# A long convolution feeding soft-MoE slots: the second stage's tables loaded whole at the start, its first loads half a step sooner, and wider scaled copies in the filter pass

## The chip, the core and the metric

One core of a Trainium2 chip runs the whole program. A time is the device time of that core in microseconds (us), from one execution. TensorE (PE) multiplies matrices into PSUM, ScalarE (ACT) and VectorE (DVE) read PSUM, GpSimd (POOL) adds and subtracts in SBUF, and SyncE (SP) issues nearly all DMA transfers of this kernel, in the order in which the program lists them. ACT issues four small loads at the start.

## What is computed

```python
x (8, 5696, 128), h (5696, 128)
Yf = rfft(x, 2S) * rfft(h, 2S)          # along the sequence
y  = irfft(Yf)[:, :S, :]                # causal long convolution per channel
x  = y.reshape(45568, 128)
logits = x @ phi                         # 32 slots
slot_input = softmax(logits, 0).T @ x    # per slot, over all tokens
slot_out   = relu(slot_input @ w1[e]) @ w2[e]      # 8 experts, 4 slots each
out = softmax(logits, 1) @ slot_out
```

All of it is float32. The filter `h` and the eight batches of `x` pass through the same forward transform: the filter is treated as group 0 and the batches as groups 1 to 8.

## The kernel before, in words

The transform of each group is done as two matrix stages with a transpose through DRAM between them. Three pipelines run side by side, each a number of steps behind the one before it. A step is one turn of the loop `for t in range(last_front + 1)` (line 547); there are 8 steps to a group (`NJ = 8`), and 72 steps of the first stage.

**Stage A** (lines 204-219) multiplies a folded piece of the input by the table `s1`. `load_x` (line 178) brings a piece of 4 x 2 columns with two DMAs into one of three buffers (`xcs`). `fold` (line 195) has POOL add or subtract the two halves into `x0` or `x1`. `stage_a(t, comp)`, called with `comp` 0 and 1 in each step, does two products into two PSUM banks out of a ring of four (line 211), ACT evicts both into `fst` (line 213; three such buffers, so a fourth eviction needs the store of the first to have landed), and SP stores `fst` to the DRAM tensor `f_g` with two DMAs (line 217). A float32 product shows as two MATMUL rows in the trace, so one `stage_a` is four rows. Each step issues four stores of `f` (180 KB each by the page) and one load of x.

**Stage B** begins nine steps after stage A (`LAG_B = NJ + 1`) and works in units of two rows of tables: 23 units to a group, up to three to a step, called from `slot_b` (line 561). `load_g(u)` (line 224) loads 256 KB of `f` into one of five `gt` buffers. `stage_b1(u)` (line 235) multiplies it by its slices of the table `wt` into a PSUM tile `bt` of two banks, `a = 0` and `a = 1` (line 244). For groups 1 to 8 DVE multiplies that by the filter's transform (`Hr`, `Hi`) into `pr`, `pi`, and adds them into `yf` (lines 265-270, two `yf` buffers). `stage_b2` (line 274) multiplies `yf` by the table `vt` into `bz`, ACT evicts into `zst`, SP stores to `z`.

For group 0, the filter, `stage_b1` takes another branch (lines 249-263). For each half `a`, ACT makes two scaled copies `ph` (128 x 128 each, one for each component `c`, line 253) from PSUM into a buffer, `pr` for `a = 0` and `pi` for `a = 1`, one of each; DVE then adds PSUM times a scale to each of them, giving `Hr` (line 255) and `Hi` (line 258). POOL negates `Hi` (line 261). The unit's PSUM tile is `bt` or `bz` by the parity of the unit; the next unit of the same parity needs both DVE halves to be through.

**Stage C** (lines 309-456) starts at step 27 and does the inverse transform's second half, the logits, both softmaxes and the slot sums. After the loop a tail handles the last pieces and the experts.

The order of the work is written out by hand (`manual_schedule`): within one step, PE, ACT, DVE, POOL and SP each get their instructions in the order of the calls: table pieces (lines 571-576), `stage_a(t, 0)`, `fold(t+1, 0)`, a unit, a unit, `load_x(t+3)`, `stage_a(t, 1)`, `fold(t+1, 1)`, a unit. `prefetch(last)` (line 554) issues the loads of `f` that are allowed: up to unit `last`, and none of group g before step 8g + 8, when all its stores have been issued. Calls in `slot_b` keep four units ahead; the very first call is at the end of step 8 (line 624).

The tables `wt` (128 x 45 x 64 float32, 1.47 MB) and `vt` (128 x 23 x 2 x 64 float32, 1.51 MB) are brought in slices of 6 and 3 rows, one slice a step: `wt` from step 7 to 14 and `vt` from step 15 to 22 (line 576), each of about 192 KB.

Of the kernel before, what the change touches and what calls it, by code (L numbers as in the profile page):

```python
# [10 lines left out]
F32 = mybir.dt.float32  # L11
AF = mybir.ActivationFunctionType
# [62 lines left out]
def kernel(  # L75
# [24 lines left out]
    nc = tc.nc  # L100
    P = 128
    B, S, D = x.shape
# [5 lines left out]
    R1, HALF, NP = S // N2, N2 // 2, N1 // 2  # L108
    CH = 4
    NJ = HALF // CH  # L110
    NU = (NP + 1) // 2
# [10 lines left out]
    t_s1, t_i1, t_w, t_v, t_turn = [  # L122
        nc.inline_tensor(t, f"tab_{n}").ap()
        for n, t in zip(("s1", "i1", "w", "v", "turn"), transform_tables(S, N1, N2, CH, X0, F0, F1))]
# [33 lines left out]
    bpool = front.enter_context(tc.tile_pool(name="bpool", bufs=1))  # L158

    s1 = apool.tile([P, 3, P], F32, name="s1", tag="s1", bufs=1)  # L160
    wt = fconst.tile([P, NP, HP], F32, name="wt")
    vt = fconst.tile([P, NU, 2, HP], F32, name="vt")
    turn = fconst.tile([P, 2, NU, 2], F32, name="turn")
# [14 lines left out]
    def load_x(c):  # L178
        if c >= (B + 1) * NJ:
            return  # L180
        g, j = divmod(c, NJ)
        src = (h if g == 0 else x[g - 1]).rearrange("(a n) d -> a n d", n=N2)
        t_ = xcs[c % len(xcs)]
        gap = N2 - CH * (2 * j + 1)
        for r in (slice(0, SPLIT), slice(SPLIT, R1)):
            v = src[r, CH * j:CH * (j + 1), :]
            v = bass.AP(tensor=v.tensor, offset=v.offset,
                        ap=[v.ap[0], [gap * D, 2], [1, CH * D]])
            nc.sync.dma_start(
                out=t_[X0 + r.start:X0 + r.stop, :, :, :].rearrange("p s n d -> p s (n d)"), in_=v)  # L190
        xs[c] = t_
# [43 lines left out]
    def stage_b1(u):  # L235
        g, i = divmod(u, NU)
        n = min(2, NP - 2 * i)
        t_ = gs.pop(u)
        tag = "bz" if g == 0 and i % 2 else "bt"
        bt = bps.tile([P, 2, 512], F32, name="bt", tag=tag)  # L240
        for a in range(2):
            r = slice(a * HP, (a + 1) * HP)
            for q in range(n):
                nc.tensor.matmul(bt[q * HP:(q + 1) * HP, a, 0:2 * D], wt[r, 2 * i + q, :],  # L244
                                 t_[r, q, :, :].rearrange("p c d -> p (c d)"),
                                 start=True, stop=True)
        r = slice(0, n * HP)
        pv = bt[r, :, 0:2 * D].rearrange("p a (c d) -> p a c d", c=2)
        if g == 0:
            for a in range(2):  # L250
                pr = bpool.tile([P, 2, D], F32, name="ph", tag="pi" if a else "pr")
                for c in range(2):
                    nc.scalar.activation(pr[r, c, :], pv[:, a, c, :], AF.Copy,  # L253
                                         scale=turn[r, 0, i, a:a + 1])
                nc.vector.scalar_tensor_tensor(  # L255
                    out=Hr[r, i, a, :], in0=pv[:, a, 1, :], scalar=turn[r, 1, i, a:a + 1],
                    in1=pr[r, 0, :], op0=AL.mult, op1=AL.add)
                nc.vector.scalar_tensor_tensor(
                    out=Hi[r, i, a, 0, :], in0=pv[:, a, 0, :], scalar=turn[r, 1, i, a:a + 1],
                    in1=pr[r, 1, :], op0=AL.mult, op1=AL.subtract, reverse1=True)  # L260
            nc.gpsimd.tensor_scalar(out=Hi[r, i, :, 1, :], in0=Hi[r, i, :, 0, :], scalar1=-1.0,
                                    scalar2=None, op0=AL.mult)
            return
        pr, pi = [bpool.tile([P, 2, 2, D], F32, name=f"p{c}", tag=f"p{c}") for c in "ri"]
        nc.vector.tensor_tensor(out=pr[r, :, :, :], in0=pv,  # L265
                                in1=Hr[r, i, :, :].unsqueeze(2).broadcast_to([n * HP, 2, 2, D]),
                                op=AL.mult)
        nc.vector.tensor_tensor(out=pi[r, :, :, :], in0=pv, in1=Hi[r, i, :, :, :], op=AL.mult)  # L268
        y_ = bpool.tile([P, 2, 2, D], F32, name="yf", tag="yf", bufs=2)
        nc.vector.tensor_tensor(out=y_[r, :, :, :], in0=pr[r, :, :, :], in1=pi[r, :, ::-1, :],  # L270
                                op=AL.add)
        prods[u] = y_
# [247 lines left out]
    LAG_B, LAG_C = NJ + 1, 3 * NJ + 3  # L520
    PER = -(-NU // NJ)
# [11 lines left out]
    AHEAD = 4  # L533
# [3 lines left out]
    nc.scalar.dma_start(out=s1[:, :, :], in_=t_s1)  # L537
    for c in range(1, 3):
        load_x(c)
    nc.scalar.dma_start(out=phi[:, :], in_=moe_phi)  # L540
    nc.scalar.dma_start(out=turn[:, :, :], in_=t_turn)
    nc.scalar.dma_start(out=i1[:, :, :], in_=t_i1)
# [4 lines left out]
    for t in range(last_front + 1):  # L547
        us = list(units(t))

        def pair(lag):  # L550
            T, half = divmod(t - LAG_C - lag, 2)
            return T if half == 0 and 0 <= T < NT else None

        def prefetch(last):
            nonlocal loaded
            while loaded < len(queue) and queue[loaded][0] <= last \
                    and queue[loaded][0] // NU * NJ + NJ <= t:
                load_g(queue[loaded][0])
                loaded += 1

        def slot_b():
            fresh = bool(us)
            if fresh:
                u = us.pop(0)
                prefetch(u + AHEAD)
                stage_b1(u)
                wait_b2.append(u)
            if len(wait_b2) > fresh:
                stage_b2(wait_b2.pop(0))

        for tab, src, first, n, k in ((wt, t_w, LAG_B - 2, NP, 2 * PER),
                                      (vt, t_v, LAG_B + NJ - 2, NU, PER)):
            p0 = k * (t - first)
            if 0 <= p0 < n:
                v = slice(p0, min(n, p0 + k))
                nc.sync.dma_start(out=tab[:, v], in_=src[:, v])
        if t < NA:
            stage_a(t, 0)
            fold(t + 1, 0)
        if pair(3) is not None:  # L580
            dispatch(pair(3))
        slot_b()
        T, U = pair(0), pair(2)
        if t == last_front:
            assert T is None and U is None and not us[1:]
            slot_b()
            stage_c2(pair(1))
            slot_b()
            assert not us and not wait_b2
            V = pair(1)  # L590
            stage_c6(V - 2)
            stage_c3(V)
            column_max(V)
            break
        rows = (lambda: None) if U is None else (lambda: stage_c4(U))
        after = None
        if T is not None:
            after = stage_c1(T, rows)
        else:
            rows()  # L600
        if pair(1) is not None:
            stage_c2(pair(1))
        if pair(5) is not None:
            stage_c6(pair(5))
        slot_b()
        if pair(-2) is not None:
            load_pair(pair(-2))
        if t < NA:
            load_x(t + 3)
        if after:  # L610
            after()
        if U is not None:
            stage_c5(U)
        if t < NA:
            stage_a(t, 1)
            fold(t + 1, 1)
        if pair(1) is not None:
            stage_c3(pair(1))
        slot_b()
        if pair(1) is not None:  # L620
            column_max(pair(1))
        if U is not None:
            softmax(U)
        if t == NJ:
            prefetch(AHEAD)
        if t == NA:
            lead.close()
            wts = inner.enter_context(tc.tile_pool(name="wts", bufs=1, side="right"))
            w1s = wts.tile([P, E, F], F32, name="w1s")
        if NA < t <= NA + E:  # L630
            nc.sync.dma_start(out=w1s[:, t - NA - 1, :], in_=moe_w1[t - NA - 1])
# [12 lines left out]
                      in_=zring[0][gap, :, :, :, :, :].rearrange("k h o n c d -> k (h o n c d)"))  # L644
# [14 lines left out]
    for q in range(Q):  # L659
        r = slice(q * NSL, (q + 1) * NSL)  # L660
        nc.gpsimd.tensor_copy(out=rep4[r, :, :],
                              in_=ident[r, r].unsqueeze(1).broadcast_to([NSL, Q, NSL]))
# [17 lines left out]
    for V in range(T, NT):  # L680
# [30 lines left out]
        else:  # L711
            for i in range(4 * (V - T - 1), min(4 * (V - T), E), 2):
                nc.sync.dma_start(
                    out=w2s[:, i:i + 2, :, :],
                    in_=moe_w2[i:i + 2].rearrange("e (p c) d -> p e c d", p=P))
# [28 lines left out]
    for g in range(EG):  # L744
        for f0 in range(0, F, FH):
# [5 lines left out]
            src = p[:, :].rearrange("p (c k) -> p k c", k=NFC)  # L751
# [5 lines left out]
    for g in range(EG):  # L757
        for k0 in range(0, NFC, 4):
            p = bank()
            for k in range(4):  # L760
# [3 lines left out]
                out=hidT[:, g, k0:k0 + 4, :], in_=p[:, :].rearrange("p (k c) -> p k c", k=4))  # L764
# [28 lines left out]
    for b in range(B):  # L793
        for w0 in range(0, NV, G4):
            n = min(G4, NV - w0)
# [10 lines left out]
            for q in range(Q):  # L806
                dst = o_[:, 0:n + lone, q, :]
                src = pq[q][:, 0:(n + lone) * D].rearrange("p (k d) -> p k d", d=D)
# [41 lines left out]
```

## Time and profile before

| what | value |
|---|---|
| median of 6 runs | 961.31 us (952.73 to 964.51) |
| the profiled execution's own time | 964.51 us |
| its span, first to last instruction | 962.7 us |
| PE busy | 849.7 us (88%) |
| DVE busy | 670.6 us (70%) |
| ACT busy | 522.3 us (54%) |
| POOL busy | 445.9 us (46%) |
| DMA | 272.51 MB, 283 GB/s over the span |
| share of the 16 DMA engines, SP's queue | 89.0% |
| first unit of stage B starts | 53.18 us |
| first unit of group 1 starts | 112.86 us |

The times in the rows below are us from the first instruction; durations in brackets after a row are how long its engine sat idle before it, and what ended that. "SPq" rows are SP issuing a DMA, not the transfer. The DMA share is the mean busy share of the 16 DMA engines. The line numbers are those of the kernel listed above.

### The profile page before, as it was taken

The page shows a single profiled execution, that of the slowest core. Times are in us where ns is not written, and L with a number is a line of the kernel's source. Part 1 is how long each engine was busy: PE and PEld are TensorE (multiplying, and loading weights), DVE is VectorE, ACT ScalarE, POOL GpSimd, SP SyncE. Part 2 cuts the span into 40 slices and gives each one's busy share as a digit, 9 for nine tenths or more (in the row PEclk, how much of TensorE's full clock was granted, in tenths as well). Part 3 has the DMA queues.
Part 4 walks back from the last instruction along what each step waited for, and adds up shares of the span by engine and source line. Part 5 has one row for each costly group of instructions (what it writes and reads, how often), then busy time and mean ns, then how long its engine had stood idle before and what let it go on. Part 6 is the DMA issues. An engine that isn't in the chain of part 4 may idle for free.

```text
span 962.7 us, 20396 instructions
## 1 busy us (share of the span) xinstructions
PE 849.7 (88%) x7220; PEld 408.0 (42%) x7220; DVE 670.6 (70%) x1140; ACT 522.3 (54%) x1068; POOL 445.9 (46%) x408
## 2 busy tenths in 40 slices
PE   6867788899899999999999899999998876787893
PEld 2322233334344444444444344444443333344883
DVE  3034577577778787888888688888889995573552
ACT  3556544455466566666665466656654444374442
POOL 5646533245465455555555555666533342462000
PEclk9979999999999999999999999999999998787865
DMA  6989899999999999999999999999989886742698
GB/s 179 277 264 265 269 311 325 308 309 288 275 290 287 298 312 300 332 297 301 315 313 275 276 312 307 311 287 321 306 275 311 276 280 194 226 162 117 235 406 334
DMA packets 174239, 272.51 MB, mean 283 GB/s; under 512 B 14982, under 2 KB 119686, under 8 KB 171253
## 3 DMA queue, kind: packets, MB, share of 16 engines
q1 hardware_dynamic: 173563, 270.86, 89.0%
q8 instruction: 58, 0.95, 0.4%
q10 hardware_dynamic: 576, 0.36, 0.2%
q14 instruction: 42, 0.34, 0.1%
HBM read 142.85 MB, written 128.21 MB: 282 GB/s over the span
## 4 chain that ended last, share of the span: by engine, by line
PE 70%; DMA 17%; issue 3%; DVE 3%; POOL 2%; SPq 1%; ACT 1%; DVEq 0%; ACTq 0%; POOLq 0%
PE bank L211 23%; PE bank L336 12%; PE bt L244 12%; PE bz L284 8%; DMA gt<-f 5%; PE bank L364 4%; DMA out_dram<-o 4%; DMA f<-fst 3%; DMA zd<-z 3%; PE bank L449 2%; PE bank L402 2%; PE bank L373 2%; POOL y L355 2%; PE bank L425 2%; PE bank L473 1%
## 5 line engine op out<-in xcount | busy, mean ns | idle before, releaser
L211 PE MATMUL bank<-x,s 128*128 128x512 f32 x576 | 285.7, 623 | 10.0 <-POOL x L200 7.9
L200 POOL TENSOR_TENSOR x<-xc 128x512 f32<-128x512 f32 x144 | 183.4, 1274 | 149.6 <-PE bank L211 83.0
L213 ACT ACTIVATE fst<-bank 128x512 f32<-128x512 f32 x288 | 167.9, 597 | 98.7 <-PE bank L211 68.0
L288 ACT ACTIVATE zst<-bz 128x512 f32<-128x512 f32 (+1 forms) x184 | 108.2, 588 | 171.6 <-PE bz L284 161.2
L265 DVE TENSOR_TENSOR pr<-bt,Hr 128x512 f32<-128x512 f32 (+1 forms) x184 | 126.9, 689 | 105.9 <-PE bt L244 102.8
L244 PE MATMUL bt<-gt,wt 64*64 64x256 f32 x1620 | 138.7, 405 | 53.4 <-DMA gt<-f 19.5
L270 DVE TENSOR_TENSOR yf<-pr,pi 128x512 f32<-128x512 f32 (+1 forms) x184 | 154.0, 837 | 6.4
L211 PEld LDWEIGHTS bank<-x,s 128*128 128x128 f32 x576 | 100.3, 193 | 133.1 <-issue 88.3
L268 DVE TENSOR_TENSOR pi<-bt,Hi 128x512 f32<-128x512 f32 (+1 forms) x184 | 125.0, 679 | 0.0
L284 PE MATMUL bz<-yf,vt 64*64 64x256 f32 x1440 | 117.3, 385 | 6.2 <-DVE yf L270 4.2
L336 PE MATMUL bank<-zc,i 128*64 128x512 f32 x480 | 118.8, 618 | 1.3 <-issue 1.3
L244 PEld LDWEIGHTS bt<-gt,wt 64*64 64x64 f32 x1620 | 44.7, 132 | 170.0 <-PE bank L211 53.5
L355 POOL TENSOR_TENSOR y<-y,op 128x512 f32<-128x512 f32 x64 | 77.4, 1210 | 70.7 <-DVE op L341 68.0
L355 POOL TENSOR_TENSOR y<-y,om 128x512 f32<-128x512 f32 x54 | 76.2, 1411 | 2.1
L410 POOL MEMSET dt<- 64x8 f32 x32 | 3.4, 106 | 157.2 <-ACT dn L413 84.3
L284 PEld LDWEIGHTS bz<-yf,vt 64*64 64x64 f32 x1440 | 54.0, 134 | 42.8 <-issue 11.6
L255 DVE SCALAR_TENSOR_TENSOR Hr<-bt,turn,ph 128x128 f32<-128x128 f32 (+1 forms) x46 | 16.1, 349 | 75.6 <-ACT ph L253 75.6
L364 PE MATMUL bank<-ident,y 109*128 109x109 f32 x512 | 60.0, 272 | 2.1 <-POOL y L355 1.4
L364 PEld LDWEIGHTS bank<-ident,y 109*128 109x128 f32 x512 | 52.5, 148 | 14.9 <-issue 11.6
L366 ACT ACTIVATE yt<-bank 128x360 f32<-128x360 f32 x128 | 51.9, 472 | 4.8 <-PE bank L364 4.8
L336 PEld LDWEIGHTS bank<-zc,i 128*64 128x64 f32 x480 | 30.0, 138 | 54.5 <-issue 48.6
L803 PE MATMUL op<-so,cT 32*128 32x128 f32 x704 | 46.8, 375 | 4.3 <-ACT o L812 3.7
(97 smaller groups left out, 896.4 us busy)
## 6 DMA issues: line engine op xcount, KB each, us to landing
f<-fst SPq DMA_DIRECT2D x288, 180.0 KB
gt<-f SPq DMA_DIRECT2D x198, 256.0 KB
z<-zst SPq DMA_DIRECT2D x176, 256.0 KB
zc<-z SPq DMA_DIRECT2D x30, 1024.0 KB
xc<-in_x_dram SPq DMA_DIRECT2D x64, 320.0 KB
out_dram<-o SPq DMA_DIRECT2D x16, 1024.0 KB
zc<-z SPq DMA_DIRECT2D x30, 416.0 KB
out_dram<-o SPq DMA_DIRECT2D x8, 768.0 KB
```

The lines of the kernel that those rows point to most:

```text
L200: nc.gpsimd.tensor_tensor(out=y_[:, :, :], in0=t_[:, 0, :, :], in1=t_[:, 1, ::-1, :], op=AL.subtract if comp else AL.add)
L211: nc.tensor.matmul(p[:, :], s1[:, tab[G], :], src[:, :, :].rearrange("p n d -> p (n d)"), start=True, stop=True)
L213: nc.scalar.activation(st[:, :, G, :], p[:, :].rearrange("p (n d) -> p n d", d=D), AF.Copy)
L244: nc.tensor.matmul(bt[q * HP:(q + 1) * HP, a, 0:2 * D], wt[r, 2 * i + q, :], t_[r, q, :, :].rearrange("p c d -> p (c d)"), start=True, sto ...
L265: nc.vector.tensor_tensor(out=pr[r, :, :, :], in0=pv, in1=Hr[r, i, :, :].unsqueeze(2).broadcast_to([n * HP, 2, 2, D]), op=AL.mult)
L268: nc.vector.tensor_tensor(out=pi[r, :, :, :], in0=pv, in1=Hi[r, i, :, :, :], op=AL.mult)
L270: nc.vector.tensor_tensor(out=y_[r, :, :, :], in0=pr[r, :, :, :], in1=pi[r, :, ::-1, :], op=AL.add)
L284: nc.tensor.matmul(bz[a * HP:(a + 1) * HP, q, 0:2 * D], vt[r, i, a, :], y_[r, a, :, :].rearrange("p c d -> p (c d)"), start=True, stop=True)
L288: nc.scalar.activation(st[:, 0:n, :], bz[:, 0:n, 0:2 * D], AF.Copy)
L336: nc.tensor.matmul(p[h_ * HP:(h_ + 1) * HP, :], i1[0:kr, tab, :], t_[0:kr, h_, o, :, q, :], start=True, stop=True)
L355: eng.tensor_tensor(out=part_, in0=part(v, 0), in1=o_[:, :, :], op=sign)
L364: nc.tensor.transpose(p[:, i * TR:(i + 1) * TR], ys[T][0:TR, k * CH + i, 0:D], ident[0:TR, 0:TR])
```

## The change

It has four parts, all of which bear on the first 170 us.

1. Both tables are loaded whole, with one DMA each, on SP's queue behind the loads of x for steps 0, 1 and 2. The sliced loads inside the loop go.
2. The first call of `prefetch`, in step 8, moves from the end of the step to the place behind `load_x(11)`. It comes before `stage_a(8, 1)` with its two stores.
3. In the filter's branch, ACT makes one scaled copy of 128 x 256 for each half instead of two of 128 x 128.
4. The copies of odd units take the two `yf` buffers (not yet in use in group 0) in place of `pr` and `pi`, so that there are four buffers.

```diff
@@ stage_b1
         if g == 0:
             for a in range(2):
-                pr = bpool.tile([P, 2, D], F32, name="ph", tag="pi" if a else "pr")
-                for c in range(2):
-                    nc.scalar.activation(pr[r, c, :], pv[:, a, c, :], AF.Copy,
-                                         scale=turn[r, 0, i, a:a + 1])
+                tag = ("pr", "yf")[i % 2] if a == 0 else ("pi", "yf")[i % 2]
+                pr = bpool.tile([P, 2, D], F32, name="ph", tag=tag, bufs=2 if tag == "yf" else None)
+                nc.scalar.activation(pr[r, :, :], pv[:, a, :, :], AF.Copy,
+                                     scale=turn[r, 0, i, a:a + 1])
                 nc.vector.scalar_tensor_tensor(
                     out=Hr[r, i, a, :], in0=pv[:, a, 1, :], scalar=turn[r, 1, i, a:a + 1],
                     in1=pr[r, 0, :], op0=AL.mult, op1=AL.add)
@@ before the loop
     for c in range(1, 3):
         load_x(c)
+    nc.sync.dma_start(out=wt[:, :, :], in_=t_w)
+    nc.sync.dma_start(out=vt[:, :, :, :], in_=t_v)
     nc.scalar.dma_start(out=phi[:, :], in_=moe_phi)
@@ in the loop
-        for tab, src, first, n, k in ((wt, t_w, LAG_B - 2, NP, 2 * PER),
-                                      (vt, t_v, LAG_B + NJ - 2, NU, PER)):
-            p0 = k * (t - first)
-            if 0 <= p0 < n:
-                v = slice(p0, min(n, p0 + k))
-                nc.sync.dma_start(out=tab[:, v], in_=src[:, v])
         if t < NA:
             stage_a(t, 0)
             fold(t + 1, 0)
...
         if t < NA:
             load_x(t + 3)
+        if t == NJ:
+            prefetch(AHEAD)
         if after:
             after()
...
         if U is not None:
             softmax(U)
-        if t == NJ:
-            prefetch(AHEAD)
```

## The prediction, on record before the changed kernel was seen

> **What bounds it now.** I read the chain that ended last, which lies on PE for 70% but has waits on DMA and stretches of "issue" in its first 180 us, then the waits, the timeline and the windows of that stretch, since the change touches nothing behind it. It falls into three stages: A alone (8 to 53 us), A with the filter's units (53 to 113 us), A with group 1 (113 to 171 us). In the last one PE keeps a step of 8.33 us and no edit touches that work: only removed table slices help DMA there, which PE's step hides.
>
> The windows of 1 us at the start (columns: PE, PEld, DVE, ACT, POOL busy, granted clock, DMA share, GB/s):
>
> ```profile
> 8.00:9.00 1.00, 1.00 (x2) 0.48 (x3) 0.89 (x3) 0.00 (x0) 1.00 (x1) 1.00 0.17 43
> 9.00:10.00 1.00, 1.00 (x3) 0.48 (x2) 0.51 (x3) 0.00 (x0) 0.12 (x1) 1.00 0.00 0
> ...
> 12.00:13.00 1.00, 1.00 (x3) 0.28 (x2) 0.00 (x0) 0.69 (x2) 0.86 (x1) 1.00 0.04 12
> ```
>
> See the hole: from 8.2 to 12.9 us DMA moves nothing, 4.7 us. From 13 us to the end of stage A its share is 0.92 to 0.95.
>
> The timeline at the turn from the first stage to the second:
>
> ```profile
> 46.46 1.10 SPq L189 DMA_DIRECT2D xc<-in_x_dram  x2
> ...
> 47.58 1.08 ACT L213 ACTIVATE fst<-bank 128x512 f32<-128x512 f32 x2 [1.59 <-DMA f<-fst]
> ...
> 48.55 3.34 SPq L230 DMA_DIRECT2D gt<-f  x5
> ...
> 53.18 1.98 PE L244 MATMUL bt<-gt,wt 64*64 64x256 f32 x16 [7.44 <-DMA gt<-f]
> ```
>
> PE stands 7.44 us for the first `gt`, issued at 48.55. The eviction at 47.58 had waited for the buffer whose store was the last of the filter's: what the load needs had landed by 47.5.
>
> Then the first filter unit, and a later step (7.58 us from 70.01 to 77.59):
>
> ```profile
> 54.38 0.62 ACT L253 ACTIVATE ph<-bt,turn 128x128 f32<-128x128 f32 x2 [5.71 <-PE bt L244]
> ...
> 55.31 0.34 DVE L258 SCALAR_TENSOR_TENSOR Hi<-bt,turn,ph 128x128 f32<-128x128 f32 x1
> 55.68 1.14 ACT L253 ACTIVATE ph<-bt,turn 128x128 f32<-128x128 f32 x4 [0.68 <-DVE Hi L258]
> ```
>
> ```profile
> 70.01 0.65 ACT L253 ACTIVATE ph<-bt,turn 128x128 f32<-128x128 f32 x2
> ...
> 71.39 1.14 ACT L253 ACTIVATE ph<-bt,turn 128x128 f32<-128x128 f32 x4 [0.74 <-DVE Hi L258]
> ...
> 72.83 0.34 DVE L258 SCALAR_TENSOR_TENSOR Hi<-bt,turn,ph 128x128 f32<-128x128 f32 x1
> ...
> 73.27 0.62 ACT L253 ACTIVATE ph<-bt,turn 128x128 f32<-128x128 f32 x2 [0.74 <-DVE Hi L258]
> ...
> 73.78 1.08 ACT L213 ACTIVATE fst<-bank 128x512 f32<-128x512 f32 x2
> ...
> 76.12 0.62 ACT L253 ACTIVATE ph<-bt,turn 128x128 f32<-128x128 f32 x2 [0.74 <-DVE Hi L258]
> ...
> 77.49 0.66 PE L244 MATMUL bt<-gt,wt 64*64 64x256 f32 x8 [1.56 <-issue]
> ```
>
> ACT's queue sets this step: it is copies, evictions and three gaps of 0.74 us without a hole between, while PE stands 1.56 + 0.27 us a step. Each gap is the second half's copy waiting for DVE to finish the **first half of the same unit**. The halves have buffers of their own (`pr`, `pi`), and at 55.68 `pi` had never been used. So this wait is not for a buffer but for the unit's PSUM tile, which ACT and DVE read by turns. (My reading; the rival below is that it is the buffer.)
>
> **The change, part by part.**
>
> *Tables whole.* 128 x 45 x 64 x 4 + 128 x 23 x 2 x 64 x 4 bytes = 2.98 MB. No row shows a load with such long rows; near are the `gt` loads landing at 56 to 58 us at 378 and 399 GB/s, the first load of x (260), and the mean of the step (about 300). I take 385: 7.7 us; ends 7.0 and 11.5. Behind the three x, these begin at about 8.1 and end at 15.8: 2.9 us past the hole. What is queued behind them on SP's queue: the stores of (0,0) issued at 12.11, x of step 3 at 13.01, and so on. The first of those (0.37 MB, 1.3 us at 285 GB/s, and some 1.4 us to complete) lands at 18.5. It frees `fst` for the fourth eviction, which now runs at 15.80: 2.7 us late; the ones after it by 2.4 and 2, as DMA's share rises a little. I carry 2.0. Two issues of 0.4 to 0.9 us each lie in SP's idle time (4.83 to 12.11).
> Here a rule speaks against the change: the Trainium skill, "DMA: Bandwidth & Descriptors", section "Queues, rings and completion order", says each DMA engine takes one queue's descriptors in ring order, so nothing overtakes the tables. If short stores could share, the start would cost about 0; by the rule, the 2.0 counted. The same page's section "Bandwidth" has 341 GB/s for 1 MB loads: 8.7 us, 1.0 more. I keep the row's 385. No run here shows which holds.
> PE in that start: it can run ahead by four banks, to 18.1, and stands about 2 us. The trace lost half the clock at 48.7, after 3 us of standing, and at 117.0, after a stretch (112 to 116) busy 0.23, 0.52, 0.03 and 0.63. "TensorE: Matmul & The Clock Gate", section "Part 1: The HAM clock gate", wants one idle window of about 3.4 us: by it the 2 us cost 0; by the row at 117, where PE was not wholly idle, a window at half clock takes one `stage_a` of 1.87 us to 3.7, up to 2.5 us in all. I take 0, the standing being shorter than either, and keep 2.5 for the range.
> Removed: slices at 39.58 and 44.26 out of the DMA-bound stage A, 0.39 MB, -1.2 us. Later ones lie beside ACT's or PE's step: 0.
>
> *First loads sooner.* SP comes to them at 47.6, after x(11), when the stores have landed, not at 48.55: 0.9; and the two stores of (8,1) no longer lie ahead in the queue: 0.37 MB, 1.2 us. Together -2.0 (-0.9 if the stores land late). Behind the five issues (3.34 us on SP) now stand the stores of (8,1), then of (9,0): out at 51 instead of 47.65. Next to want those buffers is step 10's eviction, past 58: free.
>
> Start in all: 2.0 - 1.2 - 2.0 = **-1.2** (-2.2 to +4).
>
> *Wider copy.* Rows: 128 columns 367 ns alone, 512 columns 597 ns (an eviction). Between them 256 columns are 0.444; I take 0.45, ends 0.37 and 0.60. A step of ACT before: 1.38 + 1.88 + 0.51 + 0.96 + 1.38 + 0.51 + 0.96 = 7.58, where 1.38 is pair 0.65, handoff 0.03, DVE 0.60, handoff 0.10; 1.88 holds two pairs and DVE's four operations; 0.51 is a pair less 0.11 of overlap; 0.96 two evictions. After: 0.45 + 0.04 + 0.60 + 0.10 = 1.19, then 1.71 (DVE's four now follow the shorter copy), 0.34, 0.96, 1.19, 0.34, 0.96: 6.69. **-0.89 a step** (-1.3 to -0.15). PE's work in it is 5.75, DMA's 6.14 (share 0.897 of 7.58 = 6.80, less 0.66 for a 0.20 MB slice at 299 GB/s), POOL's 2 x 1.27 + 3 x 0.85 = 5.1: all still fit.
> Steps 10 to the eviction of (15,1), 5.6 of them: 5.0. Step 9 runs at half PE clock and is PE's: 0.3.
>
> *Four buffers.* 0: the copy waits for the PSUM tile, and where the buffer of two halves before matters, that wait has already been passed. (Removing all gaps: the rival.)
>
> *The turn to group 1.* Unit 23 needs the store of (15,1) to land and a `gt` load behind it: from that eviction at 104.10 to 112.86 PE already waited 0.78 at its end. This chain is DMA and does not shrink with ACT, so the 0.89 of the last step becomes waiting; I count 0.3 for the slice at 106.05 that is gone from its way. Second stage: -(5.0 + 0.3 + 0.3) = **-5.6**.
>
> Sum -1.2 - 5.6 = **-6.8**, span 962.7 to 955.9. The profiled execution took 964.51, 3.2 over the median; taken from the median 961.31: **954.5 us**, 0.7% less. Nothing later gives it back or adds: stages A, B and C go in step numbers.
>
> **Rivals.**
>
> *The buffers were the wait* (20%). Then ACT runs free and the step falls to DMA's 6.14, or PE's 5.75: 5.6 x 1.43 + 0.6 = 8.6, with the start -9.8: 951.5. For it: ACT is only 5.4 of 7.58 busy, and a wait on DVE looks the same for a buffer and for a tile. Against: the wait at 55.68 on a fresh buffer.
>
> *The start is not hidden* (15%). Tables at 260 GB/s take 11.5 (+3.8), PE's clock falls once (+2.5), the sooner loads give 0.9 (+1.1): -6.8 + 7.4 = +0.6, 962. For: DMA is at 0.92 already after 13 us. Against: `gt` loads went at 378 and more.
>
> *Slower: the tables are a slow load* (10%). Place: SP's queue ahead of the stores at 12.11. Each us of table time past 7.7 is paid by all behind it, so the sum is T - 14.5, with T the tables' time: it turns to a loss at T = 14.5, 206 GB/s, and to 1% at 24, 124 GB/s. For: window 3 to 4 us, with the small constants, has 161 GB/s at share 0.88. That rate gives T = 18.5, +4, 965. Against: those have rows of 1.5 KB and below, here 11 KB.
>
> **How the numbers follow.** My forecast has 55%, with its own range 951 to 958.5 (copy 0.37 to 0.60, start -2.2 to +1). The range for 8 in 10 takes in the freed buffers at one end and the open start at the other: 948.5 to 962.5. Below it is a freed step at PE's 5.75, above it most of the slow tables. A measurement of this kernel can tell about 1% from no change, 9.6 us. Faster by more: half of the second case, a fifth of the first: 20%. Slower by more: the slow tables with something besides, 8%. Within: 72%.
>
> **What would show it.** In the changed profile: the DMA share between 9 and 13 us near 1; the fourth eviction at 18 to 19; the first `gt` product at 52; `ph` 128x256 near 0.45 us and still a gap of 0.7 before the second half, released by DVE `Hi`; steps of about 6.7 us; group 1's first unit near 106. Wrong if these gaps are gone, if the step stays at 7.5, if the first `gt` product is later than 55, or if the steps behind 113 us change.

## The result, and the profile after

The changed kernel takes **946.17 us** (median of 36 runs, 938.31 to 955.05), the kernel before in the same comparison 957.29 us (73 runs, 945.42 to 968.3): ratio **0.9903**, interval 0.9885 to 0.9921, so 0.8 to 1.15% faster. The forecast was 954.5 in a range of 948.5 to 962.5. The time lies below the range, and the gain is about one and a half times the sum. Two further comparisons of the same kernel gave 0.9909 (0.9868 to 0.995) and 0.9918 (0.9881 to 0.9955). The mean over all 57 runs of it is 947.1, over all 178 runs of the kernel before 957.5: **10.4 us** apart. Executions of one kernel differ by 4 to 5 us (standard deviation), and the ratio leaves out those over 1.5% above the fastest, of which the profiled execution of before and the third of the changed kernel below are two: their steps count only where others agree with them.

Part of the miss is the starting point: 961.31 came from 6 runs, and 957.29 from 73 is 4.0 lower. Taken from there, the forecast would have been 950.5 and its range 944.5 to 958.5, which holds the measured 946.17. But the gain itself, 9.3 us by the ratio and 10.4 between the means, is 2.5 to 3.6 us more than the sum. That is what the experiments had to find.

The profiled execution after took 940.51 us, its span is 938.7. The windows of 1 us at the start of the changed kernel (the same columns as in the prediction):

```profile
8.00:9.00 1.00, 0.57 (x1) 0.50 (x2) 0.89 (x3) 0.00 (x0) 1.00 (x2) 1.00 1.23 301
9.00:10.00 1.00, 1.00 (x2) 0.34 (x1) 0.51 (x3) 0.00 (x0) 0.60 (x1) 1.00 0.91 235
...
11.00:12.00 1.00, 1.00 (x2) 0.34 (x1) 0.00 (x0) 0.14 (x1) 0.00 (x0) 1.00 1.15 484
12.00:13.00 1.00, 1.00 (x3) 0.48 (x2) 0.00 (x0) 0.60 (x1) 0.65 (x1) 1.00 0.89 373
...
15.00:16.00 1.00, 1.00 (x4) 0.51 (x3) 0.00 (x0) 0.60 (x1) 0.75 (x1) 1.00 1.03 432
```

The hole is filled, and in the six windows from 10 to 16 us, while the tables move, DMA carries 373 to 484 GB/s (mean 421), more than the 385 taken: the slow tables are out. The stores behind them pay, as forecast: in the timeline of ACT, the fourth pair of evictions, at 15.80 before, waits for the first store until 18.44 us ("18 to 19" forecast). First the row of before, then that of the changed kernel:

```profile
15.80 0.60 ACT L213 ACTIVATE fst<-bank 128x512 f32<-128x512 f32 x1 [0.27 <-PE bank L211]
```

```profile
18.44 1.08 ACT L213 ACTIVATE fst<-bank 128x512 f32<-128x512 f32 x2 [0.98 <-DMA f<-fst]
```

The turn to the filter's units, and its first unit:

```profile
47.11 1.43 SPq L189 DMA_DIRECT2D xc<-in_x_dram  x2
...
49.37 2.99 SPq L230 DMA_DIRECT2D gt<-f  x5
49.41 1.09 ACT L213 ACTIVATE fst<-bank 128x512 f32<-128x512 f32 x2 [2.46 <-DMA f<-fst]
52.46 2.52 SPq L217 DMA_DIRECT2D f<-fst  x4
...
53.18 2.13 PE L244 MATMUL bt<-gt,wt 64*64 64x256 f32 x16 [5.63 <-DMA gt<-f]
...
54.38 0.47 ACT L253 ACTIVATE ph<-bt,turn 128x256 f32<-128x256 f32 x1 [3.89 <-PE bt L244]
...
55.53 0.84 ACT L253 ACTIVATE ph<-bt,turn 128x256 f32<-128x256 f32 x2 [0.68 <-DVE Hi L258]
```

The five loads now stand ahead of the step's stores, but they go out at 49.37, together with the eviction that had waited for the same stores, and the first product starts at 53.18, just where it did in the profile of before. Its sixteen rows take 2.13 us at half clock, as they did. The copy of 256 columns takes 0.47 us (0.45 taken), and the gap of 0.68 before the second half is still there.

Two units of a later step, out of a step of 6.82 us (66.52 to 73.34):

```profile
66.52 0.49 ACT L253 ACTIVATE ph<-bt,turn 128x256 f32<-128x256 f32 x1
...
67.74 0.47 ACT L253 ACTIVATE ph<-bt,turn 128x256 f32<-128x256 f32 x1 [0.73 <-DVE Hi L258]
68.11 1.07 ACT L213 ACTIVATE fst<-bank 128x512 f32<-128x512 f32 x2
...
70.29 0.84 ACT L253 ACTIVATE ph<-bt,turn 128x256 f32<-128x256 f32 x2 [0.74 <-DVE Hi L258]
...
73.34 0.49 ACT L253 ACTIVATE ph<-bt,turn 128x256 f32<-128x256 f32 x1
```

It is the same pattern as before with one wider copy in place of each pair: copy, a gap of 0.73 us for DVE's first half, copy.

**Where the time came from.** The start of the first `fst` eviction of a step marks how far a kernel has got (one execution each, us from the first instruction):

| step | before | after | after, a second execution | after, a third |
|---|---|---|---|---|
| 8 | 43.05 | 44.85 | 44.43 | 44.53 |
| 11 | 69.06 | 68.11 | 67.63 | 67.33 |
| 16 | 106.95 | 102.23 | 101.78 | 101.52 |
| 18 | 122.79 | 116.98 | 116.61 | 115.26 |
| 25 | 180.55 | 174.87 | 174.53 | 173.17 |
| 32 | 260.97 | 248.41 | 248.33 | 247.23 |
| end | 962.69 | 938.72 | 942.67 | 951.76 |

At step 25 the three executions are 5.7, 6.0 and 7.4 us ahead, against a forecast of 6.8 by then. They part in step 17, which takes 9.50, 9.58 and 8.49 us: in the first two the granted clock is at half for 3.4 us there, in the third it is not. The first unit of group 1 starts at 107.93, 107.59 and 107.24 us ("near 106" forecast). From step 25 to 32 they gain 6.9, 6.6 and 6.4 more, where "nothing later gives it back or adds". The 80.42 us of the profile of before are the longest seen for these steps; other profiles, below, put 3.4 us down to the change. From step 32 on most steps are equal to 0.1 us in all kernels (10.27, 10.73, 11.13 and 11.56 by their place in a pair of groups). What differs there (690.3, 694.3 and 704.5 us in the three executions of the changed kernel, 701.7 in that of before) falls on single steps, mostly the one where a new group's first unit waits for its `gt`, as the last section tells.

### The profile page after: what moved, and what is told of

It reads as the page before. It is cut to its first block, busy times and chain, and to the rows that moved or that the text cites. A ratio compares the mean times of both kernels' runs of the same rounds, so it can differ in the third digit from the quotient of the medians.

```text
span 938.7 us, 20316 instructions
## 1 busy us (share of the span) xinstructions
PE 841.6 (90%) x7220; PEld 404.7 (43%) x7220; DVE 669.7 (71%) x1140; ACT 515.2 (55%) x1022; POOL 446.0 (48%) x408
## 4 chain that ended last, share of the span: by engine, by line
PE 68%; DMA 18%; DVE 4%; issue 3%; POOL 2%; ACT 2%; SPq 2%; DVEq 0%; ACTq 0%; POOLq 0%
PE bank L211 22%; PE bank L336 12%; PE bt L244 11%; PE bz L284 8%; DMA f<-fst 6%; DMA gt<-f 4%; PE bank L364 4%; DMA out_dram<-o 3%; DMA zd<-z 3%; PE bank L449 2%; PE bank L373 2%; PE bank L402 2%; POOL y L355 2%; PE op L799 2%; PE bank L425 2%
## 5 line engine op out<-in xcount | busy, mean ns | idle before, releaser
L364 PEld LDWEIGHTS bank<-ident,y 109*128 109x128 f32 x512 | 51.0, 146 | 14.9 <-issue 11.6
```

What stands on the lines that cost most here:

```text
L364: nc.tensor.transpose(p[:, i * TR:(i + 1) * TR], ys[T][0:TR, k * CH + i, 0:D], ident[0:TR, 0:TR])
```

## The experiments

**Theory:** the sum holds up to step 25, and what it lacks is the bytes of the table slices taken out of steps 15 to 22, where DMA is full. **Rivals:** the copies waited for buffers; the earlier start or the wider copy is worth more than I counted; the difference is scatter. The runs below go by question. A ratio is to the kernel before on the same chip, with its interval; where means over all runs are compared, "plus or minus" is the 95% interval of their difference.

**1. One part at a time.** `wide_copy` is the kernel before with part 3 alone; `two_buffers` is the changed kernel without part 4 (its edit):

```diff
-                tag = ("pr", "yf")[i % 2] if a == 0 else ("pi", "yf")[i % 2]
-                pr = bpool.tile([P, 2, D], F32, name="ph", tag=tag, bufs=2 if tag == "yf" else None)
+                pr = bpool.tile([P, 2, D], F32, name="ph", tag="pi" if a else "pr")
```

> The kernel before with one change: each half's two 128x128 scaled copies become one of 128x256, still in one pr and one pi buffer. If the second half's copy waits for the unit's PSUM tile (my reading), the filter step falls from 7.58 to 6.8 us, as in the changed kernel, and group 1 is reached 5 to 6 us sooner: 5 us faster than before. If the four buffers did it, the step stays at 7.4 or above and the gain is under 2 us.

> The changed kernel with its copies back in one pr and one pi buffer. PSUM-tile reading: nothing moves, step 6.8, within 2 us of the changed kernel (some 9 us faster than before). Buffer reading: the step is 7.4 or above and the gain falls by 5 us or more.

`wide_copy`: 0.989 (0.9835 to 0.9946); `two_buffers`: 0.9874 (0.9829 to 0.9919), median 945.49. The filter's steps take 6.82 us in both, as in the changed kernel, against 7.58 before. So the whole shorter step is the wider copy's, and the four buffers give nothing: the rival of the freed buffers is wrong. A second set of 12 runs of `wide_copy` came out lower in gain:

> The same kernel as wide_copy, since its six times lay in two clumps (943 to 953 and 958 to 959). The wider copy reached step 18 by 7 us sooner in its profile. If all behind step 25 is chance, its median over both sets is 5 to 8 us under the kernel before; if the slices' bytes hold it back in the full DMA stages, 1 to 3 us under.

0.9972 (0.9932 to 1.0013). The two intervals overlap only barely; over all 18 runs the mean is 4.3 us (plus or minus 2.7) below the kernel before, 6.0 (plus or minus 2.8) above the changed one: between the two forecasts of the second set. By the steps, `wide_copy` is 7.3 us ahead at step 25 and `wide_copy_more`, the same kernel, 6.4. The copy alone thus brings the lead at step 25 that the whole change has there (5.7 to 7.4), and not what the change gains behind it.

**2. The tables and the sooner loads alone.** `tables_only` is the kernel before with part 1, `sooner_only` with part 2:

```diff
+    nc.sync.dma_start(out=wt[:, :, :], in_=t_w)
+    nc.sync.dma_start(out=vt[:, :, :, :], in_=t_v)
...
-        for tab, src, first, n, k in ((wt, t_w, LAG_B - 2, NP, 2 * PER),
-                                      (vt, t_v, LAG_B + NJ - 2, NU, PER)):
...
```

> The kernel before with both tables loaded whole at the start and no slices. If the start pays for the tables what the slices give back (stage A ends about 2 us later), the whole is within 2 us of before. If the 3 us or so that the changed kernel gained beyond the second stage come from the slices' bytes being gone from the full DMA stages behind, it is 3 to 5 us faster than before, and the gain shows after step 25.

> The kernel before with only the first loads of f half a step sooner. By the sum on record the first filter unit comes 2.0 us sooner than 53.18; if the loads wait for the last store of the filter whatever their place, 0 to 1 us. Its steps stay at 7.58 us.

`tables_only`: 0.9968 (0.9935 to 1.0001). Its fourth pair of evictions starts at 18.60 in place of 15.80, it is 1.4 us late at step 8 (44.45 against 43.05) and 0.1 at step 25 (180.65 against 180.55). Then it takes 74.58 us for steps 25 to 31, where the kernel before took 80.42. Its mean is 2.1 (plus or minus 4.0) below that of the kernel before beside it, which fits either expectation. `sooner_only` (one run, 958.41 beside 957.4) has its first `gt` product at 52.78 in place of 53.18: 0.4 of the 2.0 us forecast, and at step 25 it is 0.9 us behind.

**3. The changed kernel with the slices back.** Edit: part 1 undone, the rest kept.

> The changed kernel with the tables in slices again (wider copies, four buffers and the sooner first loads stay). If the tables whole do nothing in the end (they cost about 1.5 us by the end of stage A and give as much back), this is within 2 us of the changed kernel, and its first filter unit comes 0.5 to 1.5 us sooner than 53.18. If the gain beyond the second stage needs the slices gone, it is 4 us or more slower than the changed kernel.

0.9889 (0.9851 to 0.9927). By the means it is 3.0 (plus or minus 3.8) above the changed kernel, which decides neither way. Its first filter unit starts at 52.56, 0.6 us sooner than 53.18, as expected. By the steps it is ahead of the changed kernel at step 25 (173.30 against 174.87), and behind it at step 32 (250.61 against 248.41). The windows from step 25 to 32, first of the changed kernel, then of this one (columns as above):

```profile
174.90:248.40 73.50, 68.09 (x529) 28.70 (x528) 56.80 (x88) 40.09 (x73) 32.90 (x28) 1.00 1.00 320
```

```profile
173.30:250.60 77.30, 70.42 (x529) 29.39 (x528) 56.74 (x88) 40.24 (x73) 32.87 (x28) 0.96 0.99 317
```

The same 529 rows of products take 68.09 and 70.42 us of PE, since the granted clock falls to 0.96, and PE stands 1.5 us more: 3.8 us in all. The waits of the same stretches say for what PE stands (us in total, times, longest), again first of the changed kernel:

```profile
PE bt L244 <- DMA gt<-f: 2.3, 2, 1.4
```

```profile
PE bt L244 <- DMA gt<-f: 3.9, 2, 2.7
```

DVE, ACT and POOL do the same work. DMA is full in both (share 1.00 and 0.99), and no table moves in either of these windows: the last slice went in step 22.

**4. One table sliced.** `vt_sliced` and `wt_sliced` are the changed kernel with one whole load out and its slices back; each has two profiles.

> The changed kernel with only vt back in slices (steps 15 to 22), wt whole at the start. If the slices of vt in the full DMA stage lengthen steps 25 to 31 (first eviction of step 25 to that of step 32), these take 77 to 80 us as in the five kernels with slices so far (76.8 to 80.4), and the whole is 2 to 4 us slower than the changed kernel. If those 4 us were chance, or came from wt, they take 73 to 76 as in the five without.

> The changed kernel with only wt back in slices (steps 7 to 14), vt whole at the start. By the same reading these slices are out of the way long before step 25: steps 25 to 31 take 73 to 76 us, stage A ends 0 to 1 us sooner, and the whole is within 1 us of the changed kernel. If any slices cause the later loss, they take 77 or more.

> The kernel of vt_sliced once more, for a second profile: steps 25 to 31 in 77 to 80 us if the slices of vt matter, 73 to 76 if not.

> The kernel of wt_sliced once more, for a second profile: steps 25 to 31 in 73 to 76 us if only the slices of vt matter, 77 or more if those of wt do too.

`vt_sliced` 0.9907 (0.9872 to 0.9943), `wt_sliced` 0.9944 (0.991 to 0.9978). Neither the ratios nor the means part them: the means over all 12 runs lie 4.8 (plus or minus 3.9) and 3.0 (plus or minus 3.2) above the changed kernel. Steps 25 to 31 take 78.20 and 77.93 us with slices of `vt`, as expected, and 75.36 and 78.09 with slices of `wt`. The last number is a miss for the theory: in that execution one wait for a `gt` took 4.2 us, with no slice of `vt` anywhere. Over all kernels without extra loads:

| steps 25 to 31, us | kernels |
|---|---|
| `vt` in slices | before 80.42, `sooner_only` 76.78, `wide_copy` 77.98 and 79.02, `no_tables` 77.31, `vt_sliced` 78.20 and 77.93: mean 78.2 |
| `vt` whole at the start | after 73.53, 73.81 and 74.05, `two_buffers` 75.70, `tables_only` 74.58, `copies_first` 75.04, `tile_per_half` 72.94, `wt_sliced` 75.36 and 78.09: mean 74.8 |

So 3.4 us go with the slices of `vt`: all seven profiles with them take longer than eight of the nine without. The same waits and windows, over all sixteen, say where the 3.4 us are. PE stands 4.1 us for `gt` with slices and 2.4 without (means), and is busy 70.7 and 69.1 us with the same products, the granted clock being at half for 5.9 and 2.3 us. The times agree: the 24 runs of `no_tables` and `vt_sliced` together, both the changed kernel with `vt` in slices, lie 3.9 (plus or minus 2.7) above the changed kernel, and 2.4 (plus or minus 2.1) over the runs that the ratio counts. Two causes were open: the bytes themselves, or units that wait for their rows.

**5. The bytes alone.** In the changed kernel, `vt` being there, each of steps 15 to 22 loads 3 of its rows (192 KB) again, or twice 3 (the edit of `extra_load_far`):

```diff
+        again = ((15,), (18,), (20,), (15,), (18,), (0,), (3,), (6,))
+        if 15 <= t < 23:
+            for k in again[t - 15]:
+                nc.sync.dma_start(out=vt[:, k:k + 3], in_=t_v[:, k:k + 3])
         if t < NA:
             stage_a(t, 0)
```

In a first pair of kernels the rows were badly chosen, and the expectation that nothing reads them for three steps was wrong (`again` was (15,), (18,), (20,), (0,), (3,), (6,), (9,), (12,)): from step 18 on, a row of each load (5 in the load of rows 3 to 5 in step 19, for instance) was still to be read in the same step.

> The changed kernel, plus one load of 0.19 MB of the table vt in each of steps 15 to 22, into rows that no unit reads for at least three steps (the same data again, so nothing waits for it). The load alone, theory: DMA is full there, and what these bytes push back comes due in steps 25 to 31: those seven take about 78.2 us (mean of the kernels with slices of vt) in place of 75.0, the time is 3 to 5 us over the changed kernel's. Rival, the slices cost because units waited for their rows, or the difference was the scatter of single executions: steps 25 to 31 take 73 to 76, time within 1.5 of the changed kernel's. Steps 17 to 23 8.33 us by either.

> As the run with one extra load, but two of 0.19 MB a step: 3.1 MB in all. Load theory: the cost doubles or more, 81 us or more in steps 25 to 31, or the steps 17 to 23 themselves grow past 8.33 us, and the time is 6 to 10 us over the changed kernel's. Rival: steps 25 to 31 at 73 to 76, time within 2 of the changed kernel's.

> The changed kernel itself once more, as the baseline on the same chip: steps 25 to 31 at 73 to 76 us by the load theory, anywhere from 73 to 79 if that difference is only scatter; median near 946.

`extra_load` 1.0205 (1.0139 to 1.0271), `extra_load_two` 1.0198 (1.0131 to 1.0266). The waits of `extra_load` from 115 to 215 us name the cause:

```profile
PE bz L284 <- DMA vt<-tab_v: 16.9, 5, 4.0
```

Five waits of up to 4.0 us, and steps 18 to 22 of 10.48 to 13.37 us in place of 8.33. These two say nothing on bytes. They do show what a unit that waits for its row costs (some 26 us of mean time for five), and that the kernel before had no such wait: its steps 18 to 22 take 8.29 to 8.61, and its waits show none for `vt`.

The same with rows that are read no nearer than in the second step before or behind:

> The run with one extra load of 0.19 MB of vt in each of steps 15 to 22 again, with the rows chosen so that none is read in the step of its load or the one before or behind it (the earlier choice took a row that a unit read in the same step, and PE waited for it). Load theory: steps 17 to 23 stay at 8.33 us, steps 25 to 31 take about 78 in place of 74 to 75, the time is 3 to 5 us over the changed kernel's. Rival, the slices cost only where a row is late, or the difference is scatter: steps 25 to 31 at 73 to 76, time within 1.5 of the changed kernel's.

> As the run before it in this call, with two such loads a step. Load theory: 81 us or more in steps 25 to 31, or longer steps from 17 to 23, the time 6 to 10 us over the changed kernel's. Rival: 73 to 76, time within 2 of the changed kernel's.

> The changed kernel, the baseline of this call: steps 25 to 31 at 73 to 76 us, median near 947.

`extra_load_far` 0.9934 (0.99 to 0.9969), median 951.67; `extra_load_two_far` 0.9944 (0.9911 to 0.9977), 953.2; the changed kernel beside them 0.9918 (0.9881 to 0.9955), 949.78. The means over all runs are 4.6 (plus or minus 2.6) and 6.6 (plus or minus 3.7) us above the changed kernel's 57 runs: 3 to 5 and 6 to 10 were expected of the bytes, within 1.5 and 2 of the rival. Against the 8 runs beside them alone they are 3.1 (plus or minus 3.4) and 5.1 (plus or minus 4.2) above, which does not rule the rival out; both kernels together are 4.1 (plus or minus 3.3) above. By the steps (us):

| steps | after, once more | `extra_load_far` | `extra_load_two_far` |
|---|---|---|---|
| 18 to 21, each | 8.33, 8.34 | 8.34 | 8.33, 8.34 |
| 22 and 23 | 8.34, 8.34 | 8.34, 8.34 | 8.77, 11.94 |
| 25 to 31 | 73.81 | 75.61 | 75.44 |

With one load a step, the six steps from 18 on take no longer, and 25 to 31 take 75.61 us, where about 78 were expected of the bytes and 73 to 76 of the rival. That is 1.8 more than the changed kernel beside it, but within the 72.9 to 78.1 of the kernels without slices, and under all those with them: this number is the rival's. With two loads, 4.0 us are lost sooner, in steps 22 and 23, which together take 16.6 to 16.7 in every other kernel whose rows of `vt` are there in time; 25 to 31 take no longer than with one. The timeline of PE in `extra_load_two_far`, its last steps of that stage:

```profile
159.13 0.66 PE L244 MATMUL bt<-gt,wt 64*64 64x256 f32 x8 [0.37 <-DMA gt<-f]
...
163.59 0.70 PE L244 MATMUL bt<-gt,wt 64*64 64x256 f32 x8 [3.36 <-DMA gt<-f]
...
165.07 3.17 PE L211 MATMUL bank<-x,s 128*128 128x512 f32 x4
...
169.19 1.98 PE L211 MATMUL bank<-x,s 128*128 128x512 f32 x4
```

PE stands 3.36 us for a `gt`, and the next `stage_a` takes 3.17 in place of 1.98 us: the wait and then half the clock. Steps 18 to 21 had run at 8.33 or 8.34 with the same extra bytes. So extra bytes do make a `gt` late, and only some steps after they are put in. That is shown for two loads a step. That the 192 KB a step of the slices of `vt` cost their 3.4 us in the same way is the likeliest reading and not shown: one such load a step did not bring 78 us back. Nor do these runs part the bytes from the extra place that a load takes on SP.

**6. The wait on the PSUM tile, and a faster version.** `copies_first` is the changed kernel with both halves' copies ahead of DVE's four operations. `tile_per_half` gives each half of a filter unit a PSUM tile of one bank instead of sharing a tile of two:

```diff
+        if g == 0:
+            bts = [first[0].tile([P, 512], F32, name="bt", tag=f"{tag}{a}") for a in range(2)]
...
-                nc.scalar.activation(pr[r, :, :], pv[:, a, :, :], AF.Copy,
+                nc.scalar.activation(pr[r, :, :], pvs[a][:, :, :], AF.Copy,
```

> The changed kernel with both halves' copies written ahead of the four DVE operations of a unit, so that ACT and DVE take turns at the PSUM tile once per unit and not twice. PSUM-tile reading: the second half's copy follows the first with no gap, the step falls to DMA's or PE's limit, 6.0 to 6.3 us, 3 to 5 us faster than the changed kernel. If the wait were for buffers, the four of them would already be free and the step would stay at 6.8.

> The changed kernel in its own order of calls, but in group 0 each half has a PSUM tile of its own (one bank each) in place of one tile of two banks. PSUM-tile reading: the gap of 0.74 us ahead of the second half's copy goes, and the step falls to 6.0 to 6.3 us with no other edit. If the gap has another cause (the order of DVE, the scale's table), it stays and the step is 6.8 us.

`copies_first`: 0.9858 (0.982 to 0.9896); `tile_per_half`: 0.983 (0.9774 to 0.9886), median 944.19 (4 runs) beside 944.29: the two lowest, and not to be told apart. A step of `tile_per_half` (its line numbers are higher by 2 to 12):

```profile
63.66 0.66 PE L254 MATMUL bt<-gt,wt 64*64 64x256 f32 x8
...
64.40 0.84 ACT L265 ACTIVATE ph<-bt,turn 128x256 f32<-128x256 f32 x2
...
65.41 0.60 ACT L215 ACTIVATE fst<-bank 128x512 f32<-128x512 f32 x1 [0.17 <-PE bank L213]
...
66.91 1.57 ACT L265 ACTIVATE ph<-bt,turn 128x256 f32<-128x256 f32 x4
...
69.10 0.66 PE L254 MATMUL bt<-gt,wt 64*64 64x256 f32 x8
```

Four copies run on end with no wait for DVE. The gap was the tile's, as predicted, and neither buffers nor DVE's time. The two halves lie in different banks in all these kernels, so the order came with the tile and not with the bank. The steps take 5.44 to 6.4 us (copies_first 5.54 to 6.86), less on the average than the 6.0 to 6.3 expected. Over steps 11 to 14 DMA's share is 0.98, against 0.93 in the changed kernel and 0.90 in the one before, and PE is busy for 22.58 of 23.59 us: both are near their end, and which of them is the next limit is not shown. The lead of 8.4 us on the changed kernel at step 18 (108.53 against 116.98) is still 8.4 at step 25 and 9.0 at step 32; of the mean time 4.0 (plus or minus 3.9) is seen, and 3.1 (plus or minus 2.3) for `copies_first`. Where the rest goes was not settled: it is within what group turns behind step 32 scatter.

## Why the prediction was wrong

**Wider copy: right.** -0.89 a step was forecast, 0.76 measured (7.58 to 6.82), with ACT's copy 0.47 to 0.49 for 0.45. Each term was a little short: in the rows above a pair with DVE's first half takes 1.22 (66.52 to 67.74) for 1.19, and a pair's overlapped copy 0.37 (67.74 to 68.11) for 0.34.

**Four buffers: right,** and so was the reading of the gap behind it, which two runs with the tile split or the order changed show directly.

**Start: mis-sized,** -1.2 forecast, 0 between the profiles of before and after, and about -0.8 over all. The first `gt` product starts at 53.18 to 54.45 us in the three profiles with neither part 1 nor 2, and at 52.15 to 54.36 in the ten with both (means 53.8 and 53.0); one pair of profiles cannot size it. The sooner loads without the tables have it at 52.78 and 52.56 (`sooner_only`, `no_tables`): about 1.1 before 53.8, where -2.0 was counted. The tables cost 1.4 to 1.8 us by step 8 in `tables_only` and after, where one of the two early slices (0.6) has been given back: about the 2.0 of the sum.

The fourth pair of evictions came at 18.44 and 18.60, as worked out from the rule that each DMA engine takes one queue's descriptors in ring order (the Trainium skill, "DMA: Bandwidth & Descriptors", "Queues, rings and completion order"). "So nothing overtakes the tables" was my own step: the page adds that a later descriptor may finish its write before an earlier one. In these two profiles the stores did wait behind the tables. The same page's 341 GB/s for 1 MB loads ("Bandwidth"), measured on loads that GpSimd issued, was too slow here: DMA carried 421 from 10 to 16 us. The 2 us of standing that the clock was to survive did not come in the profile after: PE worked at half clock until 14.4 and was busy 12.00 of the 12 us from 13 on. In `tables_only` it stood 1.2 us, and the clock did not fall. So the 0 taken for the clock held, in part by luck.

**By step 25** these come to 5.7 to 7.4 us against 6.8. The sum held this far.

**The failed step** is "Later ones lie beside ACT's or PE's step: 0", with "only removed table slices help DMA there, which PE's step hides" and "nothing later gives it back or adds". That PE's step hides the slices is true of steps 17 to 23 (8.33 a step with and without), and false of the kernel: the slices of `vt` cost 3.4 us in steps 25 to 31, after the last of them has gone (78.2 less 74.8). Of that, 1.7 us is PE standing longer for `gt`, and 1.6 is the same products taking longer while the clock is at half. The change thus bears on more than the first 170 us, and the prediction's own sign of being wrong, "if the steps behind 113 us change", came true. What it had overlooked stood in the trace of before. From step 18 to 25 DMA's share was 0.95 to 1.00, here its two middle windows (columns as above):

```profile
131.00:147.80 16.80, 14.58 (x113) 5.73 (x113) 12.05 (x19) 8.45 (x15) 5.09 (x4) 1.00 1.00 316
147.80:164.40 16.60, 14.34 (x113) 5.71 (x112) 11.81 (x19) 8.26 (x14) 5.09 (x4) 1.00 1.00 333
```

My reading is that a queue so full takes 192 KB a step more only by getting behind, and that the loads it delays are those of the next stage, where PE runs out of `gt`. The two loads a step showed this; for the slices it stays a reading, since the changed kernel has a share of 0.95 to 1.01 in steps 18 to 23 without any slice. So the sum should have read: to step 25 about -6.4 (the mean of 5.7, 6.0 and 7.4), steps 25 to 31 -3.4, together -9.8, beside 10.4 between the means and 9.3 by the ratio.

Of the rivals, the freed buffers (20%) and the slow tables (10%) are refuted; of the unhidden start (15%) only the smaller gain of the sooner loads came true. No case of mine had a gain behind step 25. What is **not settled**: how the slices of `vt` cost what they cost, and `wt_sliced`, which by this account should lose about 1 us at most, lies 3.0 (plus or minus 3.2) us above the changed kernel, and lost 3 us in steps 25 to 31 in one of its two profiles.

## What to carry to other kernels

Where a transfer is hidden under another engine's step but the DMA share is already near 1, do not count it as free: in this kernel such transfers cost 3.4 us, and it showed only in the next stage. Cost them against the first later place where somebody waits for a load. Follow a removed transfer to the end of the full stretch, and not to the end of its own step. And when two engines take turns on one PSUM tile whose halves lie in different banks, give each half a tile of its own or put one engine's reads together, before adding buffers.

## What the runs showed of the hardware

While loads with rows of 11 KB to a partition moved, DMA carried 373 to 484 GB/s in windows of 1 us (421 from 10 to 16 us of the changed kernel), against 293 to 333 for the mix of steps 18 to 24 in the kernel before.

A wait of PE can be paid twice. In the changed kernel's timeline of PE, the first unit of group 3 waits 1.41 us, and the eight products behind it take 1.94 us, as ever:

```profile
260.86 0.66 PE L244 MATMUL bt<-gt,wt 64*64 64x256 f32 x8 [1.41 <-DMA gt<-f]
261.45 1.94 PE L336 MATMUL bank<-zc,i 128*64 128x512 f32 x8
```

In that of `extra_load_far`, the first unit of group 4 waits 2.22 us, and the same eight take 3.63:

```profile
352.13 0.66 PE L244 MATMUL bt<-gt,wt 64*64 64x256 f32 x8 [2.22 <-DMA gt<-f]
352.73 3.63 PE L336 MATMUL bank<-zc,i 128*64 128x512 f32 x8
...
356.88 1.94 PE L336 MATMUL bank<-zc,i 128*64 128x512 f32 x8
```

Its windows (columns as above) show what PE did around the wait, and the granted clock behind it:

```profile
350.00:353.00 3.00, 0.87 (x10) 0.48 (x12) 0.14 (x1) 0.55 (x1) 1.26 (x1) 0.96 0.88 261
353.00:356.00 3.00, 3.00 (x8) 0.49 (x4) 1.85 (x3) 0.60 (x1) 0.00 (x0) 0.50 1.05 382
```

The Trainium skill, "TensorE: Matmul & The Clock Gate" ("Part 1: The HAM clock gate") speaks of an idle window of about 3.4 us; here a wait of 2.22, with 0.87 us of work in the 3 us around it, was followed by half clock. No length of wait decides it, though. In the 20 traces, between 130 and 770 us, half clock follows 26 of the 28 waits of PE of 2.5 us or more, 12 of the 35 from 1.5 to 2.5, and 14 of the 336 from 0.6 to 1.5; the shortest case over 1.5 is 1.76, and a wait of 3.0 went without. This is one way in which a kernel's executions come to differ by some us: the step of a group's first unit takes 11.13 us without a wait, 12.6 with one of 1.4 and 14.99 with this one, and which of the five groups from step 33 on meets it changes from execution to execution (step 57 alone, 15.47, in the profile of before; 49 and 65, 14.86 and 14.65, in `no_tables`).

PE also begins each execution at half clock: its first rows take 1.06 us each, the later ones 0.59. (The clock's own record begins only where this ends, and the windows at 8 to 13 us show 1.00 for want of it.) How long it lasts varies: to 11.1 us in the profile of before, 14.4 in that of the changed kernel, and 10.7 to 14.9 over all, in kernels with the tables ahead and without. That is up to 2 us of PE's work in the start which no edit makes.
